# Attention over two problems: loads ordered by computed deadlines, interleaved first batches, an even output rate and a branch hint

## The chip, the cores and the metric

The kernel runs on one core of one Trainium2 chip. The metric is the device time of one execution in microseconds (us), smaller is better. Beside it stand the span of the profiled execution (first to last instruction, 1 to 2 us shorter than the time) and stretches read from its trace. Most runs of a kernel agree within some tenths of a per cent. The kernel before is looser: over the 51 runs that were made of it beside the experiments it gave 1052.9 to 1059.1 us, median 1055.7. Everything below is about effects of that size, so each experiment is timed against the kernel before in the same rounds on the same chip.

## The reference

Two independent problems A and B of the same shape, bf16 throughout: 16 batches of 144 queries with model width 448, 16 heads of width 256, and 512 keys per head.

```python
def _A_ref(x, k_cache, v_cache, wq, wo):          # B is the same with its own tensors
    q = (x @ wq).reshape(B, Sq, H, Dh).transpose(0, 2, 1, 3)
    scores = einsum("bhqd,bhkd->bhqk", q, k_cache) * (Dh ** -0.5)
    p = softmax(scores, axis=-1)
    o = einsum("bhqk,bhkd->bhqd", p, v_cache)
    return o.transpose(0, 2, 1, 3).reshape(B, Sq, H * Dh) @ wo
...
return concatenate([a, b], axis=-1)               # (16, 144, 896)
```

## The kernel before

A *unit* is one head of one batch, 512 in all: 0 to 255 are A, 256 to 511 are B. Software pipelining works in steps, one unit a step: query projection (Q), scores (S), softmax on ScalarE and GpSimd, PV, and a few matmuls of the output projection. K of the first 48 units is loaded plainly in pairs (called n) and transposed on TensorE; later K comes 16 units at a time through a transposing transfer (called k) of 4.19 MB. V comes in pairs of units (v) through a ring of nine slots, which n also uses. The weights fill SBUF so far that B's wq and wo can only be loaded once A has used its own for the last time, around unit 240 to 290: the *middle*.

All transfers are issued by SyncE in the order of two tables written by hand, with a rule for what lies between:

```python
START = ("n0 q0 x0 n1 v0 n2 q1 v1 n3 q2 n4 v2 n5 v3 q3 n6 v4 n7 v5 n8 v6 o0 n9 v7 ..." )          # cut
MID = ("k16 v127 v128 q0 v129 v130 q1 v131 q2 q3 v132 k17 v133 v134 v135 v136 v137 o0 o1 v138 o2 v139 o3 v140 o4 v141 "
       "o5 v142 o6 o7 k18")
...
def unit(U):
    pr, r = divmod(U, NU)          # problem
    b, h = divmod(r, H)            # batch after batch, 16 heads each
    return pr, b, h
...
def t_load_wq(pr, hg):             # four heads of wq at a time
    cols = slice(hg * 4 * DH, (hg + 1) * 4 * DH)
...
def t_load_x(XG):                  # two transposing transfers per group
    q.dma_start_transpose(dst[:, 0:3, :], x[:, 0:384]).then_inc(sems[sem], 16)
    ins = q.dma_start_transpose(dst[:, 3, :], x[:, 320:448]).then_inc(sems[sem], 16)
```

The output projection is a queue of matmuls from which each step takes as many as a credit allows:

```python
OP_DELAY, OP_START, OP_START_B = 2, 28, 20
OP_RATE = 1.15 * NCH * NWO / NU
...
if i >= 0:
    credit += OP_RATE
```

At the end each engine reads a flag and branches around a general path, which these inputs never need; SyncE then waits for the last stores.

```python
def body(eng):
    play(eng, eng_name, S, sems)
    eng.wait_ge(sems[flag_ev[0]], flag_ev[1])
    bad = eng.value_load(flag_ap, min_val=0, max_val=1)
    with eng.If(bad > 0):
        ...                        # the general path
    if eng_name == SP:
        drain_stores(eng, outs)
```

## Time and profile before

| | before |
|---|---|
| time, first three runs | 1056.64 us median (1056.14 to 1059.06) |
| span of the profiled run | 1055.3 us |
| first PV, PV of unit 16 | 15.75, 50.55 us |
| scores of units 48, 239, 288, 304 | 119.12, 499.55, 604.89, 638.63 us |
| last matmul, end | 1049.18, 1055.34 us |
| TensorE at half clock (after its start) | 3.4 us at 530.9 and 3.4 us at 606.0 |

The table's moments are starts of instructions in the trace, taken by unit.

### The profile page before, as it was taken

How to read it: one execution, taken by the hardware profiler on the slowest of the kernel's cores; microseconds unless marked ns; L12 is line 12 of the kernel's file. 1: busy time of each engine (PE TensorE's matmuls, PEld its weight loads, DVE VectorE, ACT ScalarE, POOL GpSimd, SP SyncE). 2: the span in 40 equal slices, each digit the busy share in tenths (PEclk: the TensorE clock that was granted, in tenths of full speed). 3: DMA queues.
4: the chain of work that ended last, by engine and by line, in shares of the span. 5: the costliest groups of instructions: out<-in, count | busy, mean ns of one | idle time of the engine just before them, and what ended most of it. 6: DMA issues, size and time to landing. Idle time of an engine off the chain costs nothing.

```text
span 1055.3 us, 32320 instructions
## 1 busy us (share of the span) xinstructions
PE 1031.0 (98%) x12376; PEld 875.0 (83%) x12376; DVE 740.9 (70%) x2039; ACT 793.9 (75%) x2365; POOL 636.6 (60%) x1030
## 2 busy tenths in 40 slices
PE   6999999999999999999999899999999999999997
PEld 6999888888888888888878788888888888888885
DVE  4776666776766777777868667677776667777775
ACT  4887667777777777878857667777877777788785
POOL 3554556656666566666746556566666666666673
PEclk9999999999999999999999999999999999999999
DMA  9999999999999999999999999999999999999960
GB/s 316 372 343 291 294 291 248 283 299 271 264 305 260 248 286 262 304 289 280 283 281 343 279 283 287 303 284 292 251 279 280 278 286 298 296 254 274 292 201 14
DMA packets 589060, 294.15 MB, mean 279 GB/s; under 512 B 500832, under 2 KB 513632, under 8 KB 588896
## 3 DMA queue, kind: packets, MB, share of 16 engines
q1 hardware_dynamic: 588896, 291.99, 110.9%
q8 instruction: 99, 1.62, 0.6%
q14 instruction: 65, 0.53, 0.2%
HBM read 161.48 MB, written 4.13 MB: 157 GB/s over the span
## 4 chain that ended last, share of the span: by engine, by line
PE 91%; DMA 5%; ACT 1%; DVE 1%; SPq 1%; issue 0%; POOL 0%; ACTq 0%; DVEq 0%
PE s_ps L1086 23%; PE ot_ps L1142 23%; PE qp_ps L1052 22%; PE op_ps L1259 19%; DMA kt_sb<-in_B_k_cache_dram 2%; DMA v_sb<-in_A_k_cache_dram 2%; PE ot_ps L1158 2%; PE s_ps L1000 1%; PE qp_ps L1000 1%; DMA wq_sb<-in_B_wq_dram 1%; PE qp_ps L1259 1%; ACT rinv_sb L1179 0%; ACT pt_sb L1096 0%; DVE ring L1194 0%; DVE qt_sb L1066 0%
## 5 line engine op out<-in xcount | busy, mean ns | idle before, releaser
L1106 POOL TENSOR_TENSOR pp_sb<-pt_sb 128x288 f32<-128x288 bf16 x512 | 384.9, 752 | 322.5 <-ACT pt_sb L1096 308.1
L1096 ACT ACTIVATE pt_sb<-s_ps 128x288 bf16<-128x288 f32 x1024 | 364.6, 408 | 184.4 <-PE s_ps L1086 177.6
L1194 DVE TENSOR_TENSOR ring<-ot_ps,rinv_sb 128x288 bf16<-128x288 f32 (+2 forms) x640 | 241.9, 394 | 150.3 <-ACT rinv_sb L1179 145.8
L1086 PE MATMUL s_ps<-qt_sb,kt_sb 128*128 128x144 bf16 x4096 | 341.3, 226 | 4.7 <-DMA kt_sb<-in_B_k_cache_dram 2.9
L1142 PE MATMUL ot_ps<-pt_sb,v_sb 128*128 128x144 bf16 x4096 | 340.3, 226 | 0.0
L1086 PEld LDWEIGHTS s_ps<-qt_sb,kt_sb 128*128 128x128 bf16 x4096 | 287.7, 98 | 56.9 <-DVE qt_sb L1066 5.6
L1179 ACT ACTIVATE rinv_sb<-ln_sb 64x144 f32<-64x144 f32 x928 | 298.3, 321 | 24.3
L1052 PE MATMUL qp_ps<-xt_sb,wq_sb 128*128 128x288 bf16 (+1 forms) x2368 | 302.3, 271 | 6.6 <-DMA wq_sb<-in_B_wq_dram 3.6
L1259 PE MATMUL op_ps<-wo_sb,ring 128*128 128x448 bf16 x1120 | 285.2, 353 | 0.0
L1052 PEld LDWEIGHTS qp_ps<-xt_sb,wq_sb 128*128 128x128 bf16 x2368 | 212.3, 98 | 81.9 <-issue 7.5
L1142 PEld LDWEIGHTS ot_ps<-pt_sb,v_sb 128*128 128x128 bf16 x4096 | 274.5, 98 | 0.5
L1111 POOL TENSOR_TENSOR p_sb<-pp_sb 128x144 f32<-128x144 f32 x464 | 227.5, 490 | 74.6 <-DVE ps_sb L1120 10.4
L1209 DVE TENSOR_REDUCE run_sb<-ot_ps 128x1 bf16<-128x144 f32 x560 | 146.5, 304 | 79.4 <-ACT ln_sb L1166 44.3
L1120 DVE TENSOR_TENSOR ps_sb<-p_sb 64x144 bf16<-64x144 f32 x464 | 158.7, 342 | 44.4 <-POOL p_sb L1111 30.3
L1066 DVE CAST qt_sb<-qp_ps 128x576 bf16<-128x576 f32 x216 | 162.1, 751 | 21.3 <-PE qp_ps L1052 17.7
L1259 PEld LDWEIGHTS op_ps<-wo_sb,ring 128*128 128x128 bf16 x1120 | 94.0, 98 | 21.2
L1166 ACT ACTIVATE ln_sb<-ot_ps 128x144 f32<-128x144 f32 x232 | 67.9, 293 | 32.6 <-PE ot_ps L1158 25.3
L1158 PE MATMUL ot_ps<-ps_sb,ones 128*128 128x144 bf16 x280 | 63.4, 226 | 0.0
L1065 DVE CAST qt_sb<-qp_ps 128x288 bf16<-128x288 f32 x80 | 35.9, 448 | 4.8 <-PE qp_ps L1052 4.3
L1008 ACT ACTIVATE kt_sb<-qp_ps 128x512 bf16<-128x512 bf16 x48 | 28.9, 603 | 7.3 <-PE qp_ps L1000 7.3
L1111 POOL TENSOR_TENSOR ps_sb<-pp_sb 128x144 bf16<-128x144 f32 x48 | 23.5, 490 | 6.9 <-PE ot_ps L1158 0.3
L1158 PEld LDWEIGHTS ot_ps<-ps_sb,ones 128*128 128x128 bf16 x280 | 27.5, 98 | 0.0
(29 smaller groups left out, 153.4 us busy)
## 6 DMA issues: line engine op xcount, KB each, us to landing
v_sb<-in_A_v_cache_dram SPq DMA_DIRECT2D x128, 512.0 KB, 7.1
v_sb<-in_B_v_cache_dram SPq DMA_DIRECT2D x128, 512.0 KB, 7.5
v_sb<-in_A_k_cache_dram SPq DMA_DIRECT2D x24, 512.0 KB, 9.6
out_dram<-ost_sb SPq DMA_DIRECT2D x36, 112.0 KB, 6.2
wo_sb<-in_A_wo_dram SPq DMA_DIRECT2D x8, 448.0 KB, 8.7
wo_sb<-in_B_wo_dram SPq DMA_DIRECT2D x8, 448.0 KB, 9.0
wq_sb<-in_A_wq_dram SPq DMA_DIRECT2D x4, 768.0 KB, 10.1
wq_sb<-in_B_wq_dram SPq DMA_DIRECT2D x4, 768.0 KB, 10.6
```

What stands on the lines that cost most here:

```text
L1052: ins = t.matmul(acc, lhsT=wq_sb[:, kc, c0:c0 + 128], rhs=xt_sb[:, kc, xo:xe + 1:max(xe - xo, 1), :], start=(kc == 0), stop=(kc == 3))
L1066: return v.tensor_copy(qt_sb[:, a:b + 1:b - a, :, :], qp_ps[:, :, 0:2 * SQ].rearrange("p e (u q) -> p u e q", u=2))
L1086: ins = t.matmul(s_ps[bank][:, (c % 2) * SQ:(c % 2 + 1) * SQ], lhsT=kt_sb[:, 2 * c + dc, ko:ko + 128], rhs=qt_sb[:, qsl, dc, :], start=(dc ...
L1096: return a.activation(pt_sb[:, psl, 2 * k:2 * k + 2, :].rearrange("p b q -> p (b q)"), s_ps[bank][:, 0:2 * SQ], AF.Exp, scale=DH ** -0.5)
L1106: return g.tensor_tensor(pp_sb[:, :, :], pt_sb[:, psl, 0:2, :], pt_sb[:, psl, 2:4, :], op=ALU.add)
L1111: return g.tensor_tensor(dst, pp_sb[:, 0, :], pp_sb[:, 1, :], op=ALU.add)
L1120: return v.tensor_tensor(ps_sb[p0:p0 + 64, sl, :], p2_sb[0:64, :], p2_sb[64:128, :], op=ALU.add)
L1142: ins = t.matmul(ot_ps[ob][:, dc * SQ:(dc + 1) * SQ], lhsT=v_sb[:, vsl, j, c * DH + dc * 128:c * DH + (dc + 1) * 128], rhs=pt_sb[:, sl, c, ...
L1179: return a.activation(rinv_sb[p0:p0 + 64, sl, :], ln_sb[h0:h0 + 64, :], AF.Exp, scale=-1.0)
L1194: ins = v.tensor_tensor(ring[:, 2 * h:2 * h + 2, r0:r0 + q1 - q0], ot_ps[ob][:, 0:2 * SQ].rearrange("p (c q) -> p c q", c=2)[:, :, q0:q1], ...
L1209: return v.tensor_reduce(run_sb[:, k, j:j + 1], ot_ps[ob][:, 2 * SQ:3 * SQ], axis=AX.X, op=op)
L1259: ins = t.matmul(acc[0:m, 0:D], lhsT=ring[:, c, col0:col0 + m], rhs=wo_sb[:, c, :], start=(c == first), stop=(c == last))
```

## The change

Its intent is to take away the waits for transfers. The hand-written tables go. A list of loads is made, each with the time at which its data is used (from a small cost list of the steps) and the time its buffer comes free, and issued in order of the latest start. The first loads become small (one head of K, one batch of x, one head of wq). The first 32 units alternate between batches 0 and 1, head by head, so that wq is asked for at half the rate. The output projection gets an even rate (1.04 for A, 1.15 for B, which starts at step 16 of B instead of 20). x comes in one transfer per group. A branch prefetch hint is set six instruction groups ahead of the final branch on each engine.

```diff
+    WQ_GROUPS = ((0, 1), (1, 2), (2, 4), (4, 8), (8, 12), (12, 16))
-    OP_DELAY, OP_START, OP_START_B = 2, 28, 20
+    OP_DELAY, OP_START, OP_RATE = 2, (28, 16), (1.04, 1.15)
+    MARGIN, HOLD = 1.0, 1.0
...
-    START = ("n0 q0 x0 n1 v0 n2 q1 v1 ...
-    MID = ("k16 v127 v128 q0 ...
...
         def unit(U):
+            if U < 2 * H:
+                return 0, U % 2, U // 2
...
+            def load(use, free, took, fn, *args):
+                made.append((at(use) - MARGIN, free, took, fn, args))
...
+            for u in range(4):
+                load(u - LT, s_min, 0.72, t_load_n, u // 2, u % 2)
...
+        todo = sorted(load_list(), key=lambda m: m[0])
+        first = [(t_load_n, (0, 0)), (t_load_x, (0,)), (t_load_wq, (0, 0, 1)), (t_load_n, (0, 1))]
+        while todo:
+            ...
+            for m in todo[:60]:
+                lo = v_lo if m[1] is None else m[1]
+                start = max(now, at(lo) + slip if lo > s_min else now)
+                latest = m[0] + slip - m[2]
+            ...                                  # earliest start, then earliest deadline
...
-                play(eng, eng_name, S, sems)
+                n = len(S.prog[eng_name]) - HINT_AHEAD
+                play(eng, S.prog[eng_name][:n], eng_name, sems)
+                ahead = eng.mark_branch_hint_location()
+                play(eng, S.prog[eng_name][n:], eng_name, sems)
...
+                branch = [k for k in here.instructions if type(k).__name__ == "InstCompareAndBranch"][-1]
+                bass.BassInstruction(branch).branch_hint(ahead)
```

The diff is cut to its core; the handling of semaphores and of x at the end of a tensor is left out.

## The prediction

> **What bounds the kernel now.** I read the page first (busy shares, slices), then TensorE's waits, then stage windows, then the chain of waits in time order, then single DMA landings.
>
> ```profile
> PE 1031.0 (98%) x12376; PEld 875.0 (83%) x12376; DVE 740.9 (70%) x2039; ACT 793.9 (75%) x2365; POOL 636.6 (60%) x1030
> DMA  9999999999999999999999999999999999999960
> ...
> q1 hardware_dynamic: 588896, 291.99, 110.9%
> ```
>
> TensorE looks full, but the DMA row is full as well until the last slices: two resources are nearly saturated. A busy PE includes pipelined ends, so I take its real cost from the chain of waits in a stage without stalls (start, duration, what):
>
> ```profile
> 702.11 0.98 PE qp_ps L1052 x8
> 703.09 0.50 PE s_ps L1086 x8
> 703.59 0.50 PE ot_ps L1142 x8
> 704.09 0.38 PE op_ps L1259 x2
> ```
>
> So a doubled query projection costs 0.98 us, scores 0.50, PV 0.50, one output matmul 0.19. Priced so (transposes 0.056 us each), all 12376 matmuls take 1021.6 us. The first starts at 4.67 us, the last at 1049.18, the span ends at 1055.3. Hence 22.9 us are lost between first and last, and 6.2 after. Summed gaps between matmul starts put the loss at 7.9 us in 0-50, 1.3 in 100-150, 12.1 in 500-650, and under 0.5 per 50 us elsewhere. TensorE's waits and the stage windows (length, busy PE, PEld, DVE, ACT, POOL, clock, DMA share, GB/s) agree:
>
> ```profile
> PE s_ps L1000 <- DMA v_sb<-in_A_k_cache_dram: 6.3, 4, 4.7
> PE qp_ps L1052 <- DMA wq_sb<-in_B_wq_dram: 3.6, 1, 3.6
> PE s_ps L1086 <- DMA kt_sb<-in_B_k_cache_dram: 2.9, 1, 2.9
> PE qp_ps L1052 <- DMA xt_sb<-in_A_x_dram: 2.3, 1, 2.3
> ```
> ```profile
> 150.00:500.00 350.00, 349.77 (x4058) 292.98 (x4057) 248.17 (x677) 270.82 (x811) 220.08 (x355) 1.00 1.15 278
> 500.00:550.00 50.00, 46.39 (x574) 39.65 (x572) 36.66 (x89) 37.33 (x112) 30.61 (x50) 0.97 1.18 292
> 550.00:600.00 50.00, 48.99 (x581) 41.46 (x580) 37.26 (x89) 36.43 (x109) 29.71 (x49) 1.00 1.17 306
> 600.00:650.00 50.00, 47.08 (x524) 38.52 (x522) 32.36 (x96) 34.78 (x104) 27.93 (x46) 0.97 1.17 294
> ```
>
> All four large waits are DMA waits: three places, start, middle (problem A gives way to B, so both weight matrices are reloaded), tail. The middle in the chain of waits:
>
> ```profile
> 522.40 7.65 DMA wq_sb<-in_B_wq_dram
> ...
> 580.09 24.67 DMA kt_sb<-in_B_k_cache_dram
> ```
>
> [...]the clock record has two stretches of 3413 ns at 0.5, one at the wq wait (near 531), one at the K wait (near 606); each costs 1.7 us more. [...]a 4.19 MB K transfer flows in 16 to 20 us (median about 18), some 230 GB/s, plain loads at about 384. [...]SyncE's branch is at 1051.56, its next instruction at 1054.85, though the last store landed at 1051.95. No run yet shows what a hint does.
>
> **The change part by part.** Matmul counts and shapes are identical in both built programs (4096 + 4096 + 1728 + 640 + 1152 + 280 + 384), so 1021.6 us stays. Only waits can move.
>
> *Start.* The first loads become one head of K, one batch of x, one head of wq. Before, two x transposes issued at 2.44 and 3.82 and landed at 8.6, behind 0.9 MB of wq; the first projection ran at 8.73. Now x is issued second, with 0.15 MB, and wq has 0.23 MB: estimate 6.2 us. Half clock then lasts to about 9.6 (before to 12.1, by the clock record). Work before the first PV is 5.5 us at full clock (4.5 units' transposes at 0.45, four projections and three score blocks at 0.50), 1.7 of which fits into the half-clock stretch; the rest puts it at about 13.0 (before 15.75): 2.7 saved. Interleaving batches 0 and 1 halves wq's rate: per 2.0 us step 0.52 MB of K and V and 0.11 of wq, 316 GB/s, not 0.75 MB, 373 GB/s, against some 335 to 370 that this stage moves. Of the 2.7 us of stalls between 16 and 33 us I leave 1: 1.7 saved, less 0.4 for small transfers. Start: 4.0 saved.
>
> *First transposed K.* It is issued after V pair 23, no longer after 22, so one slot later (two steps, 4.9 us). Before, it was issued at 94.0, landed at 115.6, was used at 119.1. From that slot to its use are 18.6 us of TensorE work: seven steps of transposes 0.45, projection 0.50, scores 0.50 and PV with its sum 0.56, 16 output matmuls (3.0) by the order of the built program, and 1.4 for what stands around it in the first and last step. The transfer needs about 20.2, the 21.6 of before less one V pair (1.4) that no longer stands ahead of it. A new wait of 1.6 us, against 1.1 lost there before: minus 0.5.
>
> *Even output rate.* In steps before 237 (K of unit 239 read, DMA free for B's first K; 500.2 us) 492 output matmuls are done, 502 before: 10 x 0.19 = 1.9 us earlier. They return later. The empty stretch of steps 269-275, where the profile shows 0.3 us waits on the evacuation every second step, is filled.
>
> *Middle.* From 500.2 us to 604.8 DMA never rests: backlog 4.2, K 17.9, plain loads (6 V, all wq) 20.6, K 19.1, plain (10 V, all wo) 23.3, K 17.4, gaps and landing about 2: 104.6. TensorE's own work for these 48 steps is 95.1 after: 48 x 1.03 for scores, PV and sums, 16 single and 16 double projections (23.7), 115 output matmuls (21.8). Before it is 92.8, with 102 output matmuls. After needs the same loads before the same K, and one V pair more (+1.4); a smaller backlog, because waves of 16 units before it last 31.5 us and no longer 30.5, gives back about 2. So DMA still needs about 104.5 us and TensorE about 95: some 9 us of waiting stay. wq now goes straight behind K, so the 3.6 us wait there goes, but it comes back at the next K, where the deficit collects. Gain of the middle by itself: about 0; the 1.9 us above is kept and 0.6 of output work is already done.
>
> *x in one transfer.* Same 256-byte packets, fewer issues; hidden. 0.
>
> *Branch hint.* SyncE would go on at once and wait for the landing at 1051.95; add 0.45 us of closing as now: end near 1052.4, 2.9 saved. I count 2.7.
>
> Sum: 4.0 - 0.5 + 1.9 + 0.6 + 2.7 + 0 = 8.7[...]. Times reported are 1.3 above the span: 1056.6 - 10 = 1046.5.
>
> **Rivals.** (1) The schedule really removes the middle's waits. For: the list is computed with deadlines, and the TensorE work is spread over it. Against: 104 us of continuous transfers against 95 of work, nothing in the diff makes them fewer. Then 12 us more go, and the time is about 1035 to 1038. (2) The start's gain is not kept: TensorE earlier by 4 us meets the same DMA at the first K and in the middle. For: DMA row full. Against: at 65-94 us the queue waits for V slots, which TensorE frees, so an earlier TensorE makes DMA earlier. Then about 1050. (3) Bunched waits: [...]the V ring runs dry behind the second K; 2 to 4 us more, 1049. (4) The hint does nothing: 1049.
>
> **Range and chances.** Each rival alone stays within 1035 to 1050; two bad ones give 1052. Range 1039.5 to 1052. Faster by over 2% needs under 1035.5, that is nearly every wait gone (1021.6 + 4 + about 3.5 of start + 3.2 of tail + 1.3 = 1033.6 is the floor): 0.07. Slower by 2%: 0.005. Same: 0.925.
>
> **What would show it.** Right: first projection near 6, first PV near 13; a wait for wq near zero; a wait of several us for K of unit 288 with a half-clock stretch; DMA without rest for about 104 us there; SyncE's gap after its branch under 0.5 us. Wrong: 500-650 without loss, plain loads or K transfers quicker than now in it, or a new wait on V behind B's second K that exceeds 3 us.

The sum came to 8.7 us, and with a further term of 1.4 us, for a shorter half clock in the middle and for the stall at 115-119 vanishing, to about 10; hence 1046.5. The 9.6 us for the end of the half clock at the start is the author's estimate: the 12.1 of the kernel before, less the 2.5 us by which the first projection was to come earlier (8.73 to 6.2). The 1.7 us for each stretch at half clock is an estimate too, half of its 3.4 us. The 2.7 us for the hint are the measured pause under the assumption that a hint takes it away.

## More of the kernel before

The stage windows of the kernel before (length, busy time and count of TensorE, weight loads, VectorE, ScalarE and GpSimd, then clock, DMA share and GB/s):

```profile
0.00:13.00 13.00, 5.35 (x51) 4.64 (x52) 4.01 (x7) 3.09 (x6) 0.70 (x6) 1.00 0.87 279
13.00:50.00 37.00, 34.99 (x568) 34.37 (x566) 25.89 (x81) 29.31 (x85) 21.53 (x36) 1.00 1.06 364
```

and from the timeline of TensorE the first query projection (start, duration; in brackets the idle time and what ended it):

```profile
8.73 1.12 PE L1052 MATMUL qp_ps<-xt_sb,wq_sb 128*128 128x144 bf16 x8 [2.34 <-DMA xt_sb<-in_A_x_dram]
```

The last column of the windows matters below: in its first 13 us the kernel moves 279 GB/s, and 364 afterwards.

## The result, and the profile after

The changed kernel takes **1054.26 us** (median of four runs, 1053.36 to 1054.68), the kernel before in the same rounds 1056.39 us. A ratio, here and below, is the mean time of one kernel's fast runs over that of the other's in the same rounds, so not quite the quotient of the medians: 0.9978, 95% interval 0.9958 to 0.9998. That is within 2%, as expected, but 2 us gained and not 10, and outside the predicted range. The two traces below lie 3.7 us apart and so show more than the medians: the profiled run of the changed kernel is the fastest of its four.

The two traces, stage by stage (us):

| stretch | before | after | difference | predicted |
|---|---|---|---|---|
| start to PV of unit 16 | 50.55 | 49.06 | -1.49 | -4.0 |
| to the scores of unit 48 (first transposed K) | 68.57 | 68.27 | -0.30 | +0.5 |
| to the scores of unit 239 | 380.43 | 379.15 | -1.28 | -1.9 |
| to the scores of unit 304 (the middle) | 139.08 | 140.21 | +1.13 | 0, and about -1.4 with the half clock |
| to the last matmul | 410.55 | 409.41 | -1.14 | -0.6 |
| to the end | 6.16 | 5.51 | -0.65 | -2.7 |
| sum | 1055.34 | 1051.61 | -3.73 | about -10 |

The page of the changed kernel, its line of busy engines:

```profile
PE 1029.9 (98%) x12376; PEld 875.8 (83%) x12376; DVE 737.7 (70%) x2039; ACT 794.1 (76%) x2365; POOL 636.2 (61%) x1030
```

Counts are those of before, as the prediction had it: only waits could move. TensorE's waits (us in total, times, longest):

```profile
PE s_ps L1112 <- DMA kt_sb<-in_B_k_cache_dram: 6.9, 1, 6.9
PE s_ps L1032 <- DMA v_sb<-in_A_k_cache_dram: 6.1, 2, 3.9
PE qp_ps L1081 <- DMA wq_sb<-in_A_wq_dram: 1.2, 2, 0.9
```

The wait for B's wq (3.6 us) is gone; that for B's K has gone from 2.9 to 6.9 us, all in one piece, in front of the scores of unit 288. The stage windows of the changed kernel, to be held against those in the prediction:

```profile
150.00:500.00 350.00, 349.72 (x4066) 292.98 (x4064) 248.73 (x678) 271.34 (x814) 220.68 (x356) 1.00 1.16 283
500.00:550.00 50.00, 49.76 (x627) 42.81 (x625) 37.37 (x95) 38.74 (x117) 31.84 (x52) 1.00 1.15 276
550.00:600.00 50.00, 45.07 (x523) 37.40 (x520) 33.35 (x83) 34.30 (x102) 27.76 (x45) 1.00 1.18 302
600.00:650.00 50.00, 47.94 (x526) 39.64 (x527) 32.05 (x95) 34.20 (x102) 27.26 (x44) 0.93 1.15 298
```

The idle time has moved from 500-550 (46.39 busy before, 49.76 now) to 550-600 (48.99 before, 45.07 now). The clock of 0.93 in the last line is one stretch of 6.8 us at half rate. It begins inside the long wait (at 599.71, the wait ends at 602.01), so 4.5 us of it hold up work. Before had two stretches of 3.4 us, each behind its wait. The chain of waits in the middle (start, duration, what) says the same: one transposing transfer sets the pace for 25 us.

```profile
576.58 25.29 DMA kt_sb<-in_B_k_cache_dram
```

The start, in the stage windows of the changed kernel:

```profile
0.00:13.00 13.00, 6.92 (x63) 6.67 (x64) 4.44 (x8) 4.10 (x7) 1.66 (x8) 1.00 0.76 215
13.00:50.00 37.00, 35.59 (x581) 35.13 (x579) 26.72 (x83) 29.84 (x87) 21.41 (x36) 1.00 1.05 369
```

and in the timelines of SyncE and then of TensorE:

```profile
3.87 0.58 SPq L1012 DMA_DIRECT2D v_sb<-in_A_k_cache_dram  x1
```
```profile
7.12 0.59 PE L1032 MATMUL s_ps<-qt_sb,v_sb 128*128 128x128 bf16 x4 [2.16 <-DMA v_sb<-in_A_k_cache_dram]
7.49 1.17 PE L1081 MATMUL qp_ps<-xt_sb,wq_sb 128*128 128x144 bf16 x8
15.02 0.66 PE L1168 MATMUL ot_ps<-pt_sb,v_sb 128*128 128x144 bf16 x8
```

The first projection is 1.2 us earlier than before, though its x and its head of wq had landed at 4.6 and 5.5 us: ahead of it in TensorE's order stand the transposes of unit 1, whose K was issued at 3.87 and landed at 7.0. The first PV is only 0.7 us earlier, and the small transfers moved fewer bytes (215 GB/s in the first 13 us, 279 before).

One profile says less about the start than it seems to. Ten profiles (this one and those of e1, e2, e4, e5, e9, e14, e15, e17 and e19 below) have the same first loads in the same order. In them the first projection starts at 7.34 to 7.60, the first V lands at 13.8 to 15.9, the first PV starts at 14.1 to 16.0 and the PV of unit 16 at 48.7 to 51.5 us (median 49.1). Single differences at unit 16 have to be held against that spread.

The end, from the instruction records of both traces (start in us, engine, what):

```
before  1051.56 SyncE branch   1054.85 SyncE next instruction   (last landing 1051.95)
after   1001.82 SyncE hint   1048.48 SyncE branch   1051.11 SyncE next instruction   (last landing 1049.07)
```

SyncE still pauses behind its branch: 2.63 us, 3.29 before.

### The profile page after: what moved, and what is told of

Same layout as the page of the kernel before. It is cut to its first block, busy times and chain, and to the rows that moved or that the text cites. A ratio compares the mean times of both kernels' runs of the same rounds, so it can differ in the third digit from the quotient of the medians.

```text
span 1051.6 us, 32329 instructions
## 1 busy us (share of the span) xinstructions
PE 1029.9 (98%) x12376; PEld 875.8 (83%) x12376; DVE 737.7 (70%) x2039; ACT 794.1 (76%) x2365; POOL 636.2 (61%) x1030
## 4 chain that ended last, share of the span: by engine, by line
PE 90%; DMA 6%; SPq 1%; ACT 1%; DVE 1%; issue 0%; POOL 0%; ACTq 0%; DVEq 0%
PE s_ps L1112 23%; PE ot_ps L1168 23%; PE qp_ps L1081 22%; PE op_ps L1284 19%; DMA kt_sb<-in_B_k_cache_dram 2%; DMA kt_sb<-in_A_k_cache_dram 2%; PE ot_ps L1184 2%; DMA wq_sb<-in_A_wq_dram 1%; PE qp_ps L1032 1%; PE s_ps L1032 1%; PE qp_ps L1284 1%; ACT rinv_sb L1205 1%; DMA v_sb<-in_B_v_cache_dram 0%; SPq L1002 0%; ACT pt_sb L1122 0%
## 5 line engine op out<-in xcount | busy, mean ns | idle before, releaser
L1146 DVE TENSOR_TENSOR ps_sb<-p_sb 64x144 bf16<-64x144 f32 x464 | 156.1, 336 | 45.8 <-POOL p_sb L1137 32.5
```

The source lines that it names most:

```text
L1146: return v.tensor_tensor(ps_sb[p0:p0 + 64, sl, :], p2_sb[0:64, :], p2_sb[64:128, :], op=ALU.add)
```

## The experiments

Two theories stand against each other. **Theory:** the middle has too many bytes for its time and the start is bound by the sum of its first transfers, so that an order of loads can only move waits; the hint does nothing. **Rivals:** the order chosen is bad in one place and a better one would gain; the half clock costs the start; the hint needs another place. All experiments are edits of the changed kernel, and all are correct unless said otherwise.

### The middle

**e2_keepw: B uses A's weights.** B's wq and wo are not loaded at all. Its output is wrong, which doesn't matter for the time.

```diff
-                    load(first_h[pr, h0], NU - H + h1 - lq(NU) if pr else s_min, 0.65 * (h1 - h0), t_load_wq, pr, h0, h1)
+                    if pr == 0:
+                        load(first_h[pr, h0], s_min, 0.65 * (h1 - h0), t_load_wq, pr, h0, h1)
-                    load(wo_use[pr, wg], wo_done[pr - 1, wg] + 1 if pr else s_min, 1.3, t_load_wo, pr, wg)
+                    if pr == 0:
+                        load(wo_use[pr, wg], s_min, 1.3, t_load_wo, pr, wg)
```

> The changed kernel, but B uses A's wq and wo: these 7.3 MB are not loaded in the middle (wrong result on purpose; same matmuls). Theory (the middle is short of DMA time: 104 us of transfers before K of unit 288 against 95 us of TensorE work): with some 20 us fewer transfers the 7 us wait and the 6.8 us at half clock (3.4 us lost) go, span 10 to 11 us shorter, about 1044 us, no excess in 500-650. Rival (the K transfers come late by themselves, because SyncE is blocked while it issues them): the wait stays above 4 us.

Measured: 1045.09 us (1043.84 to 1045.99), ratio to before 0.9894 (0.9867 to 0.9922). Its stage windows:

```profile
550.00:600.00 50.00, 50.00 (x588) 42.00 (x586) 35.73 (x91) 37.68 (x113) 30.12 (x49) 1.00 1.03 260
600.00:650.00 50.00, 49.95 (x576) 41.39 (x574) 36.60 (x104) 38.10 (x115) 30.91 (x50) 1.00 1.14 288
```

TensorE is busy throughout, at full clock, and no wait for B's K is left. From the scores of unit 239 to those of 288 it takes 98.2 us instead of 105.5. The span is 8.2 us shorter than the changed kernel's, somewhat less than the 10 to 11 expected. So the middle's loss is DMA time, and the 9 us between this run and the changed kernel are what the reload of the weights costs.

**e4_opb28: B's output projection from step 28 of B.** The deadline of wo moves back, so the list puts K of unit 288 ahead of it.

```diff
-    OP_DELAY, OP_START, OP_RATE = 2, (28, 16), (1.04, 1.15)
+    OP_DELAY, OP_START, OP_RATE = 2, (28, 28), (1.04, 1.15)
```

> The changed kernel with B's output projection starting 28 steps into B, not 16, so that K of unit 288 goes ahead of all of B's wo. Theory (DMA time is short as a sum, whatever the order): the wait at unit 288 shrinks to about 2 to 3 us, a new one appears at wo or at K of unit 304, and the time stays within 2.5 us of the changed kernel's. Rival (the order is at fault, wo ahead of K): the middle's loss of 10 us mostly goes and the time falls to 1046 us or less.

Measured: 1062.45 us (1060.64 to 1063.99), ratio 1.0063 (1.0032 to 1.0093). TensorE's first wait, and the window behind it:

```profile
PE s_ps L1112 <- DMA kt_sb<-in_B_k_cache_dram: 11.6, 1, 11.6
```
```profile
600.00:650.00 50.00, 38.41 (x431) 31.91 (x430) 26.49 (x81) 28.69 (x87) 23.27 (x38) 0.90 1.18 285
```

The wait is not at unit 288 any more (its scores come at 594.40, 97.8 us after those of 239) but at unit 304, and it is 11.6 us long. The deficit moved to the next K, as the theory has it. Three orders of the same loads thus take nearly the same time from unit 239 to 304: 139.1 us before, 140.2 in the changed kernel, 141.8 here. The loss in time was far more than I had expected (8.2 us by the medians, against 2.5). Most of it lies behind unit 304, with 6.1 us more up to the last matmul (415.5 against 409.4): 26 output matmuls more were left to do there, 4.9 us at 0.19, and 2.7 of the 10.2 us of half clock fall there.

**e9_rate: the old rate and the old start of the output projection.**

```diff
-    OP_DELAY, OP_START, OP_RATE = 2, (28, 16), (1.04, 1.15)
+    OP_DELAY, OP_START, OP_RATE = 2, (28, 20), (1.15, 1.15)
```

> The changed kernel with the old output-projection rate (1.15 throughout, B from step 20). Theory (even rate moves 10 output matmuls out of the time before unit 239 and 13 into the stretch up to unit 288, where TensorE would wait): unit 239 reached 2 us later, wait at 288 about as long or longer, since K lands 105 us after unit 239 either way: 1.5 to 2.5 us slower than the changed kernel. Rival (the even rate is without effect): same within 0.7 us.

Measured: 1059.78 us (1059.67 to 1060.72), ratio 1.0036 (1.0021 to 1.0051). TensorE's waits:

```profile
PE s_ps L1112 <- DMA kt_sb<-in_B_k_cache_dram: 7.8, 1, 7.8
...
PE ot_ps L1168 <- DMA v_sb<-in_B_v_cache_dram: 3.8, 1, 3.8
```

From unit 48 to unit 239 it takes 381.12 us, 1.97 more than the changed kernel: ten output matmuls at 0.19, exactly the term of the prediction. From 304 to the last matmul 1.1 us more, six of them. But the middle loses another 3.3 (239 to 304 in 143.5 us against 140.2), with a wait for V behind B's second transposed K, 10.2 us of half clock (5.7 of them inside the wait for the next K), and three waits of 0.3 to 0.4 us for VectorE to copy a query projection out. So within the new order the even rate is worth about 5.5 us, twice what was expected. The order of loads is computed from the rate, so both changed here; which of them made the wait for V was not taken apart.

**e5_warmmid: 30 spare matmuls ahead of the scores of unit 288.** They fill the wait with work that is meant to keep the clock up, and their result is overwritten.

```diff
+        def t_spin(U, n):
+            ...
+                for _ in range(n):
+                    ins = t.matmul(s_ps[bank][:, 0:D], lhsT=ones[:, :], rhs=wo_sb[:, 0, :], start=True, stop=True)
+            S.add(PE, e, reads=[("ones", 1), (("wo", 0), 1)], writes=[(("sp", bank), -U)], ...)
...
             for u in of_step(ls, i):
+                if u == 288:
+                    t_spin(u, 30)
                 t_s(u)
```

> The changed kernel with 30 spare matmuls (448 columns, about 5.7 us in all, into a score bank that the next real matmul overwrites) put before the scores of unit 288. Theory (the wait for K of unit 288 is DMA time and stays, but the 7 us idle halves the clock for 6.8 us, which costs 3.4 us more): scores of 288 start when they did (K lands near 602), no half-clock stretch after it, span 3.4 us shorter, about 1051 us. Rival (the spare work only comes on top, or the clock falls anyway): same time or up to 6 us longer.

Measured: 1053.10 us (1051.24 to 1055.09), ratio 0.9968 (0.9954 to 0.9982). What is left of the wait:

```profile
PE s_ps L1112 <- DMA kt_sb<-in_B_k_cache_dram: 1.2, 1, 1.2
```

No half clock from 12.1 to 1049.8 us, and the 16 units from 288 on take 32.6 us instead of 34.7. That is 2.1 of the expected 3.4 us: the expectation halved the whole stretch of 6.8 us, but only the 4.5 us behind the wait hold up work, which makes 2.3. By the medians (of different rounds) the time is 1.2 us shorter, and the two intervals overlap. In the profiled run K landed later (239 to 288 in 107.0 us), so part of the gain was eaten there. In the changed kernel 6.8 us of half clock went with the wait of 6.9 us; with the wait filled down to 1.2 us, none followed here.

### The start

**e3_n01: K of unit 1 issued second.** So that the transposes of unit 1 do not hold up the first projection.

```diff
-        first = [(t_load_n, (0, 0)), (t_load_x, (0,)), (t_load_wq, (0, 0, 1)), (t_load_n, (0, 1))]
+        first = [(t_load_n, (0, 0)), (t_load_n, (0, 1)), (t_load_x, (0,)), (t_load_wq, (0, 0, 1))]
```

> The changed kernel with the second unit's K (256 KB) issued second, ahead of x and wq. Theory (in the changed kernel the first projection waited, in TensorE's order, behind the transposes of unit 1, whose K was issued fourth at 3.87 us and landed at 7.0, while x and wq had landed at 4.6 and 5.5): first projection at about 6.3 us and not 7.49, first PV about 1 us earlier, span 1 us shorter[...]. Rival (the start is bound by the sum of early transfers): first PV unchanged within 0.3 us.

Measured: 1054.35 us (1053.64 to 1054.95), ratio 0.9985 (0.9959 to 1.0012). TensorE's wait for x and wq takes the place of that for unit 1's K: first projection 7.23 instead of 7.49, first PV 15.10 instead of 15.02, PV of unit 16 at 48.69 instead of 49.06. The order of the first four matters neither for the first PV nor for the time. That their sum does is not shown by this run.

**e7_bigstart: the first transfers in the old sizes.** The interleaved batches stay.

```diff
-    WQ_GROUPS = ((0, 1), (1, 2), (2, 4), (4, 8), (8, 12), (12, 16))
+    WQ_GROUPS = ((0, 4), (4, 8), (8, 12), (12, 16))
...
-            for u in range(4):
-                load(u - LT, s_min, 0.72, t_load_n, u // 2, u % 2)
-            for G in range(2, NNAT):
+            for G in range(0, NNAT):
...
-        first = [(t_load_n, (0, 0)), (t_load_x, (0,)), (t_load_wq, (0, 0, 1)), (t_load_n, (0, 1))]
+        first = [(t_load_n, (0,)), (t_load_x, (0,)), (t_load_wq, (0, 0, 4)), (t_load_n, (1,))]
```

> The changed kernel with the first transfers in their old sizes (two units of K in one, two batches of x in one, wq by four heads), the interleaving of the two batches kept. Theory (what the small first transfers gain for the first projection they lose again, because SyncE issues them too slowly: 215 GB/s moved in the first 13 us against 279 before, and the first V lands at 14.4 us, after 12.1 before): DMA at 270 GB/s or more in 0-13, first projection back at about 8.7 us, first V landed by 12.7, first PV within 0.7 us of the changed kernel's 15.0, fewer wq waits later, time within 1.5 us of the changed kernel's. Rival (small first transfers are what gained at the start): first PV 16 us or later and span longer by over 1 us.

Measured: 1054.30 us (1052.70 to 1057.35), ratio 0.9987 (0.9967 to 1.0007). Its wait for wq, and its first window:

```profile
PE qp_ps L1081 <- DMA wq_sb<-in_A_wq_dram: 3.9, 1, 3.9
```
```profile
0.00:13.00 13.00, 4.35 (x36) 3.73 (x37) 3.56 (x6) 2.68 (x4) 0.70 (x6) 1.00 0.86 278
```

The first projection is 2.8 us later (10.27) and the first PV 3.0 us (17.98), both outside the spread of the ten profiles. The PV of unit 16 is only 1.1 us later (50.13), which lies inside it: the larger transfers bring more bytes early on (278 GB/s in the first 13 us against 215), and no later wait for wq is left. The first V landed at 14.29 and not by 12.7 as expected. So the small first loads do start TensorE earlier; how much of that is left at unit 16, one profile cannot say. Both sides were partly right; in the time nothing remains.

**e8_nointer: batch after batch again.** The interleaving alone is undone.

```diff
-            if U < 2 * H:
-                return 0, U % 2, U // 2
```

> Changed kernel, with batches 0 and 1 of problem A no longer interleaved (all 16 heads of batch 0 first, as before); small first transfers, deadlines and even rate are kept. Theory (the interleaving halves what wq asks of the DMA in the first 35 us and so takes the waits for wq away there): new waits for wq of 1.5 to 3 us in sum between 15 and 40 us, the PV of unit 32 1 to 3 us later, time 1 to 2.5 us longer than the changed kernel (about 1055.5 to 1057). Rival (the start is bound by the sum of what must come in, the order of units does not alter that much): within 0.7 us of the changed kernel.

Measured: 1057.62 us (1056.19 to 1059.28), ratio 1.0024 (1.0006 to 1.0043). A wait and a window:

```profile
PE qp_ps L1079 <- DMA wq_sb<-in_A_wq_dram: 2.6, 1, 2.6
```
```profile
13.00:50.00 37.00, 33.97 (x530) 33.68 (x528) 24.34 (x77) 27.43 (x79) 19.71 (x33) 0.95 1.08 335
```

A wait for wq of 2.6 us at 16 us is followed by a half-clock window (3.4 us from 19.1 on, hence the 0.95), and the PV of unit 16 comes at 51.99, 2.9 us later and just beyond the spread of the ten profiles. The time is 3.4 us longer by the medians (of different rounds), more than expected, and the intervals of the two ratios do not overlap. The interleaving is the part of the start that pays, and without it the kernel would be no faster than before.

**e6_warmstart: spare matmuls in the first 7 us.** TensorE is idle for much of that time, and its clock is at half until 12.6 us (in the trace of the changed kernel eight score matmuls take 0.96 us at 10.27 and 0.50 at 12.85).

```diff
+                if u == 0:
+                    t_spin0(0, 22)
+                if u == 1:
+                    t_spin0(1, 22)
                 t_tr(u, 0)
```

(`t_spin0` is 22 matmuls of the ones into a free bank.)

> Changed kernel, with 22 spare matmuls ahead of each of the first two transposed units, so that TensorE is busy from about 2 us on and its clock is full earlier than at 12.6 us. Theory (the start is bound by DMA: the first V pair lands at 14.4 us and the first PV starts at 15.0): the clock is full by about 8 us, the first PV stays within 0.6 us of 15.0, the time within 0.6 us of the changed kernel. Rival (the half clock costs the start): the PV of unit 16 1 to 1.7 us earlier (from 49.1 to 47.5 or 48), the time that much shorter.

Measured: 1053.53 us (1053.19 to 1056.70), ratio 0.9989 (0.9969 to 1.0008). The clock is full from 4.8 us on, the first PV comes at 14.63 (15.02 without), the PV of unit 16 at 49.51 (49.06). With the clock full, TensorE stands idle for 1.7 us in all between its first projection and its first PV, and that PV follows 0.2 us behind the landing of the first V (14.39). So behind the clock stands a second bound, what comes in, and the faster clock does not shorten the start as a whole. The profiled run is one of the two long ones, and its waits show why it is long:

```profile
PE s_ps L1112 <- DMA kt_sb<-in_B_k_cache_dram: 4.8, 1, 4.8
...
PE s_ps L1112 <- DMA kt_sb<-in_A_k_cache_dram: 2.5, 1, 2.5
```

The first transposed K of A came 2.5 us late in this execution (0.3 us in that of the changed kernel), and a half-clock window followed at 120.8 us. The next wait, in the middle, is 2 us shorter in return.

**e11_actq: five of the first loads from ScalarE's queue.**

```diff
+        early = (("n", (0, 1)), ("n", (1, 0)), ("n", (1, 1)), ("n", (2,)), ("v", (0,)))
+        for kind, args in early:
+            queue = [ACT]
+            {"n": t_load_n, "v": t_load_v}[kind](*args)
+        queue = [SP]
```

> The changed kernel with five early loads (second unit's K, K of units 2 to 5, V of units 0 and 1) issued from ScalarE's queue before its first activation, the others from SyncE's as before. Theory (the start is bound by the rate at which one queue issues small transfers): over 280 GB/s in 0-13 us, first V landed by 11 us, first PV at about 12.5 to 13.5 and not 15.0, span 1.5 to 2.5 us shorter. Rival (bound by the DMA engines or the cold clock): first PV within 0.5 us of 15.0.

Measured: 1055.72 us (1055.50 to 1057.94), ratio 1.0001 (0.9984 to 1.0018). Its wait:

```profile
PE qp_ps L1081 <- DMA wq_sb<-in_A_wq_dram: 5.2, 1, 5.2
```

First projection at 11.34, first PV at 18.30, PV of unit 16 at 50.44. My expectation was wrong. More bytes came in (255 GB/s over the first 13 us) and the first V landed at 11.29, but K of later units arrived at the cost of the head of wq that the first projection waited for. That is what a second queue cost here, where one of the transfers was urgent: 11.34 us instead of 7.49.

### The end

**e1_nohint: the hint removed.**

```diff
-                ahead = eng.mark_branch_hint_location()
-                bass.BassInstruction(branch).branch_hint(ahead)
```

> The changed kernel without the prefetch hint. Theory (the hint prefetches nothing: in the changed kernel SyncE still pauses 2.6 us after its branch): time as the changed kernel's, 1054.3 +- 1.5 us, and SyncE's pause after the branch 2.6 to 3.3 us. Rival (the hint shortened that pause by the 0.7 us seen between the two traces, and more on other engines): pause back at 3.3 us on SyncE and span longer by 0.7 us or more from the last matmul to the end.

Measured: 1054.30 us (1053.52 to 1055.18), ratio 0.9981 (0.9954 to 1.0007). SyncE's pause is 2.68 us (2.63 with the hint), from last matmul to end 5.53 us (5.51). The hint does nothing that these times show. Over the fourteen profiles with a hint in which SyncE has nothing else to wait for, its pause is 2.63 to 3.82 us; without it, 2.68 here and 3.29 before. The fetching of instructions appears as transfers on queues of their own. The page (queue, kind: packets, MB, share) has the same two lines for the kernel before, the changed kernel and this run:

```profile
q8 instruction: 99, 1.62, 0.6%
q14 instruction: 65, 0.53, 0.2%
```

With the hint nothing more is fetched: 164 transfers either way. In the changed kernel no such transfer begins within 2 us behind SyncE's hint (1001.82), and nine begin between the first engine's branch (1044.94) and the end, two of them 1.0 and 1.3 us behind SyncE's own branch. Which engine a transfer belongs to is not told. This run and e3_n01 are also the nearest to a repetition of the changed kernel: 1054.30 and 1054.35 us.

**e15_hint2: the hint two groups ahead instead of six.** Not timed in rounds.

```diff
-    STORE_LAG, HINT_AHEAD = 12, 6
+    STORE_LAG, HINT_AHEAD = 12, 2
```

> Changed kernel, the hint two instructions (groups) ahead of each engine's end instead of six. In the changed kernel SyncE executed its hint 46.7 us ahead of the branch, the other engines 1.8 to 12.1 us. Theory (the hint fetches nothing for this branch, at whatever distance): SyncE's hint then stands under 10 us ahead of its branch, the pause after the branch stays between 2.4 and 3.4 us. Rival (46.7 us is too early, what was fetched is gone again): the pause falls under 1 us, last matmul to end from 5.5 to about 3.5 us.

Measured: one run of 1056.92 us. SyncE's hint came 28.4 us ahead of its branch and not under 10 as I had expected, since its last groups are stores that wait; those of the other engines came 1.6 to 8.8 us ahead. SyncE's pause is 2.90 us, from last matmul to end 5.78. In the changed kernel the hint stood 1.8 us (TensorE) to 46.7 us (SyncE) ahead of its branch, and the pauses behind were 4.0 and 2.6 us; no distance that was tried helped. The length of this one run comes from its start (a 2.1 us wait for wq and a half-clock window at 26.7).

**e14_nobranch: no branch at all.** The flag is still read. The result is correct for these inputs, but the general path is gone, so this is no candidate.

```diff
-                with eng.If(bad > 0):
-                    ...
                 if eng_name == SP:
                     drain_stores(eng, outs)
```

> Changed kernel with the branch to the general path and its hint taken out altogether (the flag is still computed and read into a register; with these inputs the general path is never entered, so the result stays correct; as a kernel it would be wrong for inputs outside its limit, which is why it is only an experiment). Theory (the 2.6 us between SyncE's branch and its next instruction are the taken branch itself, which the hint does not shorten): SyncE goes on at once after its register reads and waits for the last landing, which was 4.0 us before the... that is 3.0 us after the last matmul; last matmul to end falls from 5.5 to 3.3 to 3.8 us, the time by 1.7 to 2.2 us to about 1052.3. Rival (the pause is something else that stands at the end of the program, such as the closing of the engines, and the branch lies beside it): last matmul to end stays at 5.2 to 5.6 us.

Measured: 1051.97 us (1051.50 to 1053.20), ratio 0.9971 (0.9954 to 0.9988). From the instruction records:

```
1046.72 last matmul   1049.01 SyncE last register instruction   1049.52 last landing   1049.53 SyncE goes on   1049.99 end
```

From last matmul to end it takes 3.27 us instead of 5.51. The page counts 97 and 59 instruction transfers here, eight fewer, and none of them begins at the end. So the pause goes with the taken branch, and eight instruction transfers go too; taking it out is worth 2.2 us. That the transfers cause the pause is not shown. The prediction had the sum nearly right and the means wrong.

**e17_actstore: the last store behind ScalarE's branch.** If the branch can't be made shorter, it can be taken earlier: SyncE branches as soon as its other stores are issued, and ScalarE issues the last one behind its own branch.

```diff
+                prog, late = S.prog[eng_name], S.prog[SP][-1:]
+                if eng_name == SP:
+                    prog = prog[:-1]
...
-                        drain_stores(eng, outs)
+                        drain_stores(eng, early)
...
+                if eng_name == ACT:
+                    play(eng, late, eng_name, sems)
```

(`early` is `outs` without that store.)

> Changed kernel, the last store issued from ScalarE's queue past its own branch, so that SyncE takes its branch while VectorE still evacuates the last chunk, and only waits for the landing afterwards (the branch and the general path stay). Theory: SyncE's branch moves from 2.4 us after the last matmul to about 0.5 us after it, its pause ends about 3.2 us after the last matmul, the last store lands about 3.6 us after it; last matmul to end falls from 5.5 to 4.0 to 4.4 us, the time by 1.1 to 1.5 us to about 1052.9. Rival (another engine's pause takes its place: TensorE's is 3.9 us from 1045.2): last matmul to end stays above 5 us.

Measured: 1056.17 us (1054.78 to 1056.42), ratio 1.0007 (0.9994 to 1.0021), by the medians (of different rounds) 1.9 us slower than the changed kernel. From the records:

```
1047.17 last matmul   1047.19 SyncE branch   1048.87 ScalarE issues the store, for 2.73 us   1053.81 landed   1054.33 end
```

SyncE's branch came as early as planned, but the issue took 2.73 us (3.02 in e18_best below). In e11_actq ScalarE issued its transfers in 0.41 to 0.66 us.

**e19_spstore: both last stores behind SyncE's own branch.** The same edit with `[-2:]` and SyncE in place of ScalarE.

```diff
+                prog, late = S.prog[eng_name], S.prog[SP][-2:]
...
+                if eng_name == SP:
+                    play(eng, late, eng_name, sems)
```

> Changed kernel, SyncE takes its branch as soon as the flag is there (about 0.9 us before the end of the last matmul) and issues its last two stores past it. Theory (the branch costs about 2.7 us once, and an engine that has issued transfers before issues one in 0.35 us behind it): SyncE resumes about 2.6 us after the last matmul, both stores are issued by 3.4 us and landed by about 5.0 us after it, last matmul to end falls from 5.5 to 4.6 to 5.4 us. Rival (any store behind a branch pays the slow issue of 2.7 us seen on ScalarE): last matmul to end over 6 us, time as in the run with ScalarE's store.

Measured: 1054.33 us (1053.36 to 1055.65), ratio 0.9987 (0.9971 to 1.0002). SyncE branches at 1045.31, goes on 2.79 us later and issues its two stores in 0.36 and 0.42 us. The slow issue is thus not that of any store behind a branch; it was ScalarE's, whose only transfer this was. Why that one is slow is not shown. From last matmul to end 5.17 us, 0.34 less than in the changed kernel: the stores now start later by what the branch took.

### What adds up

**e13_warmboth** joins the edits of e5_warmmid and e6_warmstart; **e18_best** adds that of e17_actstore, **e20_spwarm** that of e19_spstore.

```diff
 e13_warmboth = changed kernel + t_spin0(0, 22) + t_spin0(1, 22) + t_spin(288, 30)
 e18_best     = e13_warmboth + last store behind ScalarE's branch
 e20_spwarm   = e13_warmboth + last two stores behind SyncE's branch
```

> Changed kernel with the spare matmuls at both places: 22 and 22 at the start, 30 ahead of the scores of unit 288. A candidate for the best version. By the DMA theory 1052.8 to 1053.6 (that of the middle alone was 1053.1, the start adds nothing); by the rival for the start 1051.5 to 1052.3. In both no half clock between 15 and 1050 us.

> Spare matmuls at the start (22 and 22) and ahead of unit 288 (30), and the last store past the branch on ScalarE's queue. If the gains add up: 1.7 us (that of the two clocks together by the medians, 1052.5) and 1.3 us of the end: about 1051.2, between 1050.2 and 1052.2. No half clock between 15 and 1040 us; last matmul to end 4.0 to 4.4 us.

> The same with the spare matmuls at the start (22 and 22) and ahead of unit 288 (30). If the theory of the store holds, 0.2 to 0.9 us under that with the matmuls alone (median 1052.5, on another chip): 1051.5 to 1052.5, with single runs up to 1058 where the transfers of the middle run slowly. If the rival holds, 1053 to 1055.

Measured:

| | median, range (us) | ratio to before | the single runs |
|---|---|---|---|
| e13_warmboth | 1052.51, 1051.56 to 1058.02 | 0.9984 (0.9961 to 1.0008) | 1051.6, 1058.0, 1051.8, 1053.2, 1052.0, 1053.1 |
| e18_best | 1055.18, 1052.20 to 1058.12 | 0.9996 (0.9976 to 1.0016) | 1058.1, 1052.2, 1056.7, 1053.7, 1058.0, 1052.2 |
| e20_spwarm | 1054.72, 1051.80 to 1059.61 | 0.9987 (0.9962 to 1.0012) | 1056.1, 1053.4, 1059.6, 1052.7, 1056.1, 1051.8 |

Three times the same: some runs at 1052, others 4 to 7 us longer. The profile of e13_warmboth fell on a short run (span 1049.7 us), that of e18_best on a long one (1056.3 us). TensorE's wait for the first transposed K in the former, and two waits in the latter:

```profile
PE s_ps L1112 <- DMA kt_sb<-in_A_k_cache_dram: 1.2, 1, 1.2
```
```profile
PE s_ps L1112 <- DMA kt_sb<-in_A_k_cache_dram: 2.7, 1, 2.7
...
PE qp_ps L1081 <- DMA wq_sb<-in_B_wq_dram: 1.7, 1, 1.7
```

Neither run waits for B's K; from the scores of unit 239 to those of 288 the short one takes 104.9 us with the spare matmuls in it, the long one 107.5. In the long one the first K is late by 1.5 us more, a half-clock window follows at 118.6, and the transfers of the middle are late again. So it is the pace of the transfers that differs. Part of that goes with the spare matmuls at the start: in the four profiles that have them (e6, e13, e18, e20) the first transposed K took 21.3 to 22.8 us from issue to landing, in the fourteen others with the new order 19.9 to 20.9. Why it does, and why executions of one program differ, is open: the single runs of e18_best and e20_spwarm go up and down in turn, and no run here tells what alternates. No version is shown to be better than the changed kernel: e5_warmmid has the lowest ratio of those that keep the general path, with an interval that overlaps.

## Why the prediction was wrong, point by point

**What bounds the kernel** was right: DMA full (a share of 1.15 from 150 to 500 us, 1.16 after), TensorE nearly full (98% of the span), and only waits to move. The counts of matmuls stayed.

**Middle, right in its mechanism.** "DMA still needs about 104.5 us": from 239 to 288 the changed kernel took 105.5 us, before 105.3, and eleven profiles with this middle lie between 104.2 and 106.5. "TensorE about 95" was some 3 us too low: without the weights (e2_keepw), and with no wait for a transfer, it was 98.2, so 6.9 us of waiting were left and not 9. "It comes back at the next K": 3.6 us for wq went, 4.0 came at K, and in e4_opb28 it moved on to the K after that.

**Even rate, right in sign and size.** 1.9 us were counted up to unit 239; e9_rate against the changed kernel shows 1.97, before against after 1.28. The "0.6 of output work already done" measured 1.1. What the term left out is that the old rate, put into the new order, would have cost another 3.3 us in the middle.

**The step that failed most: "Start: 4.0 saved".** It measured 1.5 us in the two profiles (1.4 against the median of the ten). It had the first projection at 6.2 and the first PV at 13.0; they came at 7.49 and 15.02. Two terms were mis-sized. The estimate took x and wq as what the projection waits for and overlooked unit 1's K ahead of it in TensorE's order: 1.3 us. And "half clock then lasts to about 9.6": it lasted to 12.6. In this trace TensorE works without a pause from the first projection to the first PV, 5.1 us of it at half clock. In this stretch eight score matmuls take 0.96 us instead of 0.50 (10.27 and 12.85), so about half the time is lost at half clock. The two terms then make up 0.6 and 1.5 us (an estimate from these moments), which is the 2.0 us missing at the first PV.

Mending either gained little, because the transfers stand close behind. Moving unit 1's K (e3_n01) gained nothing, and a full clock from 4.8 us on (e6_warmstart) brought the first PV 0.4 us. The first V landed at 14.4. Up to and with it 2.8 MB are loaded (from the shapes), as many as before, when it landed at 12.1; so "less 0.4 for small transfers" was too little. In none of the ten profiles did it land before 13.8, and the first PV followed 0.1 to 0.8 us behind it. The part "1.7 saved" by the interleaving is not shown to be too large: undoing it cost 2.9 us at unit 16.

**The second: "Branch hint, 2.7".** It brought nothing (e1_nohint, e15_hint2). The 0.65 us by which the end of the two profiles differs is not the hint's: without it the same stretch took 5.53 us. The reading beneath was sound: the pause goes with the taken branch, and without it the end comes 2.2 us earlier (e14_nobranch). What failed is the step from "the branch is costly" to "the hint takes the cost away", for which the text itself said that no run showed it.

**The third, small: the 1.4 us for a shorter half clock in the middle and for the stall at 115-119.** That stall had been counted already, in the minus 0.5 for the first K. As for the clock, what counts is the half clock behind the wait for K of unit 288, and it got longer: 3.4 us before, 4.5 of the 6.8 now, which costs 0.6 us more. Two more output matmuls (42 against 40) add 0.4. That is the 0.9 us by which the stretch from 288 to 304 got longer (33.75 to 34.68), and most of the +1.1 us of the middle. How long a wait must be for a half clock to go with it is not shown: waits of 3.6 and 2.9 us in the kernel before had one of 3.4 us each, a wait of 2.1 us (e15_hint2, 24.45 to 26.54) was followed by one, and one of 3.8 us (e9_rate, 562.59 to 566.40) by none, the clock of 550 to 600 being 1.00.

**The first K** was priced +0.5 us and measured -0.3; with the spare matmuls of e6_warmstart it was 2.5 us late, so the sign of one profile says little.

**The range.** Rivals 3 and 4 each had a part of it: 3 the bunched wait with its half clock, 4 that the hint has no effect. Rival 2 had the start's gain lost later; in fact most of it was never made. The text allowed for two bad ones, 1052. Three at once are 1054. A quarter of the predicted gain stood on the one thing that no profile showed, and another part on small transfers that were assumed to flow like large ones. Besides, the 1056.64 us of the first three runs lie 0.9 us above the median of the later 51, so a part of what is measured as gain against them is chance: held against those, the changed kernel and its two near repetitions (1054.3 us) gain 1.4 us.

## What to carry to other kernels

When the DMA is full over a stretch, first sum its bytes against the work that must hide it: here each of three orders moved the wait to another transfer (139.1, 140.2 and 141.8 us from unit 239 to 304), and only fewer bytes took it away (unit 239 to 288 in 98.2 us, not 105.5). Of a stretch of half clock, count only what lies behind the wait (here 4.5 of 6.8 us). Count a gain at the start where the pipeline has filled (here after 16 units), not at the first instruction, and over several profiles (here it spread by 2.8 us), and give no gain to a hint or a switch that no run has shown to work.
